# Another order of the matmuls in an attention step, V stored token by token, early stores on ScalarE's queue

## The chip, the cores and the metric

The kernel runs on one core of a Trainium2 chip. The metric is device time in microseconds (us) for one launch. A profiled execution adds a trace: when each instruction ran on TensorE (PE, with its weight loads PEld), VectorE (DVE), ScalarE (ACT), GpSimd (POOL), and when SyncE (SP) issued DMAs. PEclk in its rows is the share of TensorE's full clock that was granted.

## The reference

One transformer block on 2048 tokens of width 512, in float32: a layer norm whose scale and shift come from a condition vector, softmax attention with 32 heads of 16 elements, a second layer norm, and a GELU layer of width 1792.

```python
mod = (silu(c) @ w_mod).reshape(1, 6, 1, -1)
sa, ca, ga, sb, cb, gb = ...
h = layernorm(x) * (1 + ca) + sa
q, k, v = split_heads(h @ wqkv)                     # 32 heads of 16
p = softmax(einsum("bhqd,bhkd->bhqk", q, k) * 16 ** -0.5)
x = x + ga * (einsum("bhqk,bhkd->bhqd", p, v) @ wo)
h = layernorm(x) * (1 + cb) + sb
x = x + gb * (gelu(h @ w1 + b1) @ w2 + b2)
```

## The kernel before

Tokens come in four row blocks of 512 (`NB`, `TB`), heads in eight groups of four (`NG`). A unit `u` is one group of heads with one row block of queries, 32 in all. Every operand of a matmul is split into a rounded part ("hi") and the rest ("lo"), and the products hi·hi, lo·hi and hi·lo are added; for the heads these three products lie under each other in 48 rows of a tile (`KR`), and two further rows add minus the row's maximum, so that the exponent of a score is ready when its matmul ends. A tile has two row halves: rows 0 to 49 belong to one head (a = 0), rows 64 to 113 to another (a = 1).

The order of the work on each engine is written out by hand; the program is issued in just that order.

1. **First part** (`for b in range(NB)`, L489 to L525). Per row block: layer norm, transposes, the q and k projections of the first two groups (`proj_qk`, L294), and half of the V projections (`proj_v`, L323). Results are stored to DRAM, since the attention reads them in another layout. In `proj_qk`, ScalarE copies the hi part, VectorE subtracts the lo part, and for every second block the sums and differences of neighbouring k blocks (`pm`, `pmh`) are made and finished on GpSimd. The stores (L314, L319, L332) are issued on SyncE's queue at once, in order with SyncE's loads. The tiles `parts` and `pmh` share a ring of three buffers. Between the blocks stand the products with the modulation weights (`mod_rows`), whose 1 MB pieces SyncE loads (`load_wm`, L139).
2. **Projections with maxima** (`for n, (k, b, w) in enumerate(items)`, L550). 8 more V items and 24 q or k items, each of 12 matmuls. From the third item on (`FILL0 = 2`) four visits are spread over an item's matmuls; each visit makes two slots of `pair_slot` (L402): two matmuls for the two row halves into a bank each of the ring `mx`, then either an absolute value on ScalarE (V slots) or a sum with minimum on VectorE (U slots). This gives the row maxima of units 0 to 7 from sums and differences of k (`kpm`). Slots that the items don't reach are made after the loop (L582).
3. **Steps** (`for s in range(NS)`, L805). 512 steps; a step is one unit and 128 of its keys. PSUM's eight banks are then the rings `sc` (4), `mx` (3) and `pv` (1). A step does what `ORDER[s % 2]` lists: X0 to X3 are the scores of the four heads (`exp_step`, L794: one matmul in row half j % 2 into a bank of `sc`, then an exponent on ScalarE); P is the product of the step before with V (`pv_step`, L629: four matmuls in four column groups, eight rows in the trace); M0 and M1 are each a bank of maxima for a later unit (`next_max`, `max_bank`, L389: one matmul in row half 0 or 1 into a bank of `mx`, then a maximum over 512 scores on VectorE). `EXTRA` puts a further M at the end of some steps. Units 8 to 31 get their maxima so. When a unit's 64 banks are done, `max_rows` (L429) transposes the result through one more bank of `mx`, and a DMA brings it into the score's extra rows.
4. **Rest** (L834 to the end). Output projection, second layer norm, and the GELU layer.

## Time and profile before

| | us |
|---|---|
| median of 3 runs (lowest to highest) | 1953.41 (1939.52 to 1955.21) |
| the profiled execution | 1953.68 |
| its span | 1951.9 |
| busy PE / DVE / ACT / POOL | 1908.6 / 1444.5 / 1345.3 / 256.3 |
| first part, up to the first matmul of maxima | 0 to 112.31 |
| projections with maxima | 112.31 to 304.75 |
| slots after the loop, up to the first score | 304.75 to 318.98 |
| steps | 318.98 to 1594.6 |
| rest | 1594.6 to 1951.9 |

Busy is the time in which an engine ran an instruction of the program. Matmuls overlap in the array, so a busy PE need not be PE at its peak; in the steps what counts is how many matmuls share it. In the rows of a timeline the first number is the start, the second how long the row lasted; "x3" joins three like instructions, and the bracket at the end holds the engine's idle time before it and what ended it. A row of the view by stages gives for each engine the busy time and the number of instructions, then the granted clock, the DMA engines' busy share and GB/s.

### The profile page before, as it was taken

The numbers are of one execution on the slowest core, as the hardware profiler recorded it, in microseconds if no ns is written. First come the engines' busy times: TensorE is split into PE (matmuls) and PEld (weight loads), VectorE is DVE, ScalarE is ACT, GpSimd is POOL, SyncE is SP. The second block draws the span as 40 slices with busy tenths as digits, with TensorE's granted clock in tenths as the row PEclk, the third lists the DMA queues.
The fourth block names the chain that finished last, engine by engine and source line by source line (L and its number), as shares of the span: only waits on it lengthen the run. The fifth ranks groups of instructions, "written<-read, shape, count | busy, mean of one in ns | idle before, by whom it ended". The sixth has DMA issues, their size and how long they took to land.

```text
span 1951.9 us, 29242 instructions
## 1 busy us (share of the span) xinstructions
PE 1908.6 (98%) x10586; PEld 988.4 (51%) x10586; DVE 1444.5 (74%) x2591; ACT 1345.3 (69%) x2552; POOL 256.3 (13%) x259
## 2 busy tenths in 40 slices
PE   8879999999999999999999999999999999999998
PEld 6535554444444444444444444444444357878887
DVE  6349997588888888888888888888888549566553
ACT  3357776588888888888888888888888853122222
POOL 3200000010000000000000000000001006455562
PEclk9979996699999999999999999999999999999999
DMA  8796445220401301220140011011001315343331
GB/s 248 199 135 145 106 148 93 42 49 26 67 23 29 67 21 24 56 40 21 27 72 20 21 40 26 21 35 31 21 21 58 100 62 173 96 126 92 115 119 54
DMA packets 116800, 139.96 MB, mean 72 GB/s; under 512 B 33104, under 2 KB 67920, under 8 KB 114896
## 3 DMA queue, kind: packets, MB, share of 16 engines
q1 hardware_dynamic: 116656, 138.10, 29.5%
q8 instruction: 83, 1.36, 0.3%
q14 instruction: 61, 0.50, 0.1%
HBM read 104.28 MB, written 33.77 MB: 71 GB/s over the span
## 4 chain that ended last, share of the span: by engine, by line
PE 88%; DVE 5%; DMA 4%; issue 2%; POOL 1%; ACT 0%; SPq 0%; DVEq 0%; POOLq 0%; ACTq 0%
PE pv L635 26%; PE mx L397 22%; PE sc L802 14%; PE sc L290 12%; PE mx L867 5%; PE mx L414 4%; PE pv L867 2%; PE sc L742 1%; DVE mxs L399 1%; DMA wmod<-in_w_mod_dram 1%; DMA kt<-kpm 1%; DMA rb<-rden 1%; DMA kpm<-pmh 1%; PE mx L742 1%; DVE cp L425 0%
## 5 line engine op out<-in xcount | busy, mean ns | idle before, releaser
L803 ACT ACTIVATE p<-sc 128x512 f32<-128x512 f32 x2048 | 1058.4, 606 | 210.8 <-PE sc L802 191.0
L399 DVE TENSOR_REDUCE mxs<-mx 128x1 f32<-128x512 f32 x1536 | 968.9, 684 | 235.5 <-PE sc L802 169.3
L635 PE MATMUL pv<-p,vg 128*32 128x512 f32 x4096 | 557.3, 616 | 0.0
L802 PE MATMUL sc<-qst,kq 50*128 50x512 f32 x1024 | 315.0, 448 | 0.4 <-DVE mr L438 0.4
L397 PE MATMUL mx<-kt,qmx 48*128 48x512 f32 x768 | 312.3, 449 | 1.4
L397 PE MATMUL mx<-kq,qmx 48*128 48x512 f32 x768 | 305.3, 434 | 2.0 <-DVE mxs L399 0.8
L802 PE MATMUL sc<-qst,kt 50*128 50x512 f32 x1024 | 304.9, 430 | 0.0
L397 PEld LDWEIGHTS mx<-kt,qmx 48*128 48x128 f32 x768 | 143.2, 193 | 251.6 <-DVE mxs L399 207.6
L397 PEld LDWEIGHTS mx<-kq,qmx 48*128 48x128 f32 x768 | 138.4, 185 | 244.5 <-DVE mxs L399 218.1
L846 ACT ACTIVATE g<-sc,b_c 128x512 f32<-128x512 f32 x56 | 38.6, 690 | 237.1 <-PE sc L290 228.5
L425 DVE CUSTOM_DVE_ANT_0 cp<-mx,cp 128x512 f32<-128x512 f32 x256 | 164.3, 685 | 33.8 <-PE mx L414 31.3
L440 POOL CAST m<-mr 16x128 fp32r<-16x128 f32 x32 | 9.1, 285 | 1301.6 <-DVE mr L438 1301.6
L421 ACT ACTIVATE cp<-mx 128x512 f32<-128x512 f32 x256 | 140.3, 597 | 57.5 <-PE mx L414 55.3
L635 PEld LDWEIGHTS pv<-p,vg 128*32 128x32 f32 x4096 | 81.6, 108 | 180.1 <-issue 168.5
L802 PEld LDWEIGHTS sc<-qst,kq 50*128 50x128 f32 x1024 | 147.3, 192 | 37.2 <-ACT p L803 21.4
L802 PEld LDWEIGHTS sc<-qst,kt 50*128 50x128 f32 x1024 | 142.7, 185 | 14.2
L850 DVE TENSOR_TENSOR glo<-g,ghi 128x512 fp32r<-128x512 f32 x56 | 60.1, 1073 | 94.8 <-ACT ghi L849 94.8
L414 PE MATMUL mx<-kt,qmx 48*128 48x512 f32 x512 | 102.7, 472 | 11.2 <-DMA qmx<-qk 11.0
L671 POOL TENSOR_TENSOR w1l<-w1r,w1h 128x512 fp32r<-128x512 f32 x56 | 76.8, 1372 | 152.6 <-DVE w1h L670 132.5
L290 PE MATMUL sc<-hThi,w 128*128 128x512 f32 x256 | 82.7, 434 | 3.1 <-DVE hThi L258 3.1
L673 POOL TENSOR_TENSOR w2l<-w2r,w2h 128x512 fp32r<-128x512 f32 x56 | 81.1, 1449 | 6.5 <-DVE w2h L672 6.1
L414 PEld LDWEIGHTS mx<-kt,qmx 48*128 48x128 f32 x512 | 43.9, 192 | 62.9 <-issue 23.7
(147 smaller groups left out, 1646.0 us busy)
## 6 DMA issues: line engine op xcount, KB each, us to landing
qk<-parts SPq DMA_DIRECT2D x32, 512.0 KB
w1r<-in_B_w_dram SPq DMA_DIRECT2D x56, 256.0 KB
w2r<-in_B_w_dram SPq DMA_DIRECT2D x56, 256.0 KB
qmx<-qk SPq DMA_DIRECT2D x192, 64.0 KB
qst<-qk SPq DMA_DIRECT2D x192, 64.0 KB
wmod<-in_w_mod_dram SPq DMA_DIRECT2D x6, 1024.0 KB
kq<-qk SPq DMA_DIRECT2D x24, 256.0 KB
kt<-qk SPq DMA_DIRECT2D x24, 256.0 KB
```

The source lines that it names most:

```text
L290: te.matmul(ps, p, q, start=i == 0, stop=i == len(terms) - 1)
L397: te.matmul(ps, qmx[u][rows, p, qc * P : (qc + 1) * P], kst[u // NB][rows, p, kr * TB : (kr + 1) * TB], start=True, stop=True)
L399: ve.tensor_reduce(mxs[u][:, p, a, qc, kr : kr + 1], ps, axis=AX.X, op=ALU.max, negate=True)
L414: te.matmul(ps, qmx[u][rows, p, qc * P : (qc + 1) * P], kpm[u // NB][rows, p, t0 : t0 + TB], start=True, stop=True)
L421: ac.activation(vabs[n, a], ps, AF.Abs)
L425: ve.tensor_tensor_reduce(v, ps, v, -0.5, 3.0e38, ALU.add, ALU.min, mxs[u][:, p, a, qc, r : r + 1])
L635: te.matmul(cur_pv[0][32 * j : 32 * (j + 1)], vg[g][:, kc, j * VW : j * VW + 32], pt.pop((s, j)), start=kc == 0, stop=kc == NKC - 1)
L671: gp.tensor_tensor(alo, a, ahi.bitcast(F32), op=ALU.subtract)
L673: gp.tensor_tensor(blo, b, bhi.bitcast(F32), op=ALU.subtract)
L802: te.matmul(ps, k[r0 : r0 + KX, p, kc * P : (kc + 1) * P], q[r0 : r0 + KX, p], start=True, stop=True)
L803: ac.activation(pb, ps, AF.Exp, scale=SCALE)
L867: te.matmul(acc[qb][t], p[:, sl], q, start=f == 0 and n == 0, stop=f == NF - 1 and n == 2)
```

## The change

- `ORDER` is rewritten. Both versions have, in two steps, eight X, two P and three M for each row half; they stand in another order.
- The extra M of `EXTRA` now stands behind X1 instead of at the end of the step, one step earlier, and takes its bank from the ring `sc` (written "m0", "m1") instead of `mx`.
- The stores of the first part go to ScalarE's queue (`st[0] = ac`), until item 1 of the second loop, from where they go to SyncE's again. Each is issued one projection later than it was: `proj` keeps the store (`rest`) and issues it after the next projection's own instructions.
- `parts` and `pmh` share four buffers instead of three.
- V lies in DRAM as token, group, element instead of group, token, element. A store of 128 tokens is one run of 2656 bytes for each partition, before eight of 332; the load of a group (`load_v`) is 16 runs of 332 bytes for each partition, before one of 5312.
- `load_qm(0)` stands ahead of the loads of the first `kpm` tile instead of behind them; the second half of that tile is loaded in one place behind the loop; the second `kpm` tile is loaded at item 8 instead of 3.
- Visits begin at item 4 (`FILL0 = 4`), and odd items hold five visits.

```diff
-FILL0 = 2
+FILL0 = 4
-ORDER = ("X0 X1 M0 X2 M0 X3 P M1".split(), "X0 X1 M1 X2 M1 X3 P M0".split())
-EXTRA = {5: 0, 13: 1, 17: 1, 25: 0}
+ORDER = ("X0 X1 M1 X2 M0 X3 P M1".split(), "X0 X1 X2 M0 M0 X3 P M1".split())
+EXTRA = {4: "m0", 12: "m1", 16: "m1", 24: "m0"}
...
-    v_d = dram.tile([NG, P, NKC, VG], F32, name="v")
+    v_d = dram.tile([P, NKC, NG, VG], F32, name="v")
...
+    st = [ac]
...
-        parts = tpool.tile([P, 2, TB], FR, tag="parts", name="parts", bufs=3)
+        parts = tpool.tile([P, 2, TB], FR, tag="parts", name="parts", bufs=4)
...
-            sy.dma_start(qk_d[w][k][:, :, b * TB : (b + 1) * TB].rearrange("a p t -> p a t"), parts.bitcast(F32))
+            st[0].dma_start(qk_d[w][k][:, :, b * TB : (b + 1) * TB].rearrange("a p t -> p a t"), parts.bitcast(F32))
...
-                    sy.dma_start(kpm_d[:, :, t0 : t0 + TB].rearrange("a p t -> p a t"), pmh[i].bitcast(F32))
+                    st[0].dma_start(kpm_d[:, :, t0 : t0 + TB].rearrange("a p t -> p a t"), pmh[i].bitcast(F32))
...
-        return lambda: sy.dma_start(v_d[:, :, b * 4 + t, :].rearrange("g p e -> p g e"), v)
+        return lambda: st[0].dma_start(v_d[:, b * 4 + t], v)
...
-        ps = bank_mx()
+        ps = bk()
...
+    rest = lambda: None
+    def proj(f, *args):
+        nonlocal rest
+        r = f(*args)
+        rest()
+        rest = r
...
             kpm[0], kpm[1] = kts
+            load_qm(0)
             build_k(kts[0], kpm_d, 0, 0, 2 * TB)
...
-        proj_qk(b, 0, 1)()
-        proj_qk(b, 0, 0)()
+        proj(proj_qk, b, 0, 1)
+        proj(proj_qk, b, 0, 0)
         if b == NB - 1:
-            build_k(kts[0], kpm_d, 0, 2 * TB, S)
-            load_qm(0)
             break
...
-    close(acm)
+    build_k(kts[0], kpm_d, 0, 2 * TB, S)
...
-        sy.dma_start(vg[g], v_d[g])
+        sy.dma_start(vg[g], v_d[:, :, g])
...
     for n, (k, b, w) in enumerate(items):
-        if n == 3:
+        if n == 1:
+            close(acm)
+            st[0] = sy
+        if n == 8:
             build_k(kts[1], kpm_d, 1)
...
-            fill = [lambda rest=rest: (rest(), visit()), visit, visit, visit]
+            fill = [lambda rest=rest: (rest(), visit())] + [visit] * (3 + n % 2)
...
-        order = ORDER[s % 2] + [f"M{a}" for k, a in EXTRA.items() if k % 16 == kc and (k < 16 or u < 4)]
+        order = list(ORDER[s % 2])
+        for k, tok in EXTRA.items():
+            if k % 16 == kc and (k < 16 or u < 4):
+                order.insert(2, tok)
...
-                new += next_max(int(tok[1]))
+                new += next_max(int(tok[1]), bank if tok[0] == "m" else bank_mx)
```

More of the change, by code (lines that the diff above doesn't have):

```diff
@@ L307, in proj_qk @@
             pm = [apool.tile([P, TB], F32, tag="h32", name="pm", bufs=3) for _ in range(2)]
-            pmh = [tpool.tile([P, 2, TB], FR, tag="parts", name="pmh", bufs=3) for _ in range(2)]
+            pmh = [tpool.tile([P, 2, TB], FR, tag="parts", name="pmh", bufs=4) for _ in range(2)]
             for i, op in enumerate((ALU.add, ALU.subtract)):
@@ L387, in block_kernel, with max_bank @@
     mi = [NU1 * NM, NU1 * NM]
-    def max_bank(u, i, a):
+    def max_bank(u, i, a, bk):
         if u not in left:
@@ L447, in max_rows, with next_max @@
         return rest
-    def next_max(a):
+    def next_max(a, bk=bank_mx):
         u, i = divmod(mi[a], NM)
@@ L456, in next_max @@
         mi[a] += 1
-        max_bank(u, i, a)
+        max_bank(u, i, a, bk)
         return [] if left[u] else [max_rows(u)]
@@ L513, in block_kernel @@
             mrow = mod_rows(wms)
-        proj_v(*vitems.pop(0))()
+        proj(proj_v, *vitems.pop(0))
         ev = ln1_t(b + 1, xn)
         ev()
-        proj_v(*vitems.pop(0))()
+        proj(proj_v, *vitems.pop(0))
         if b == 1:
@@ L523, in block_kernel @@
         if b == 0:
-            proj_v(*vitems.pop(0))()
-            proj_v(*vitems.pop(0))()
-    close(acm)
+            proj(proj_v, *vitems.pop(0))
+            proj(proj_v, *vitems.pop(0))
+    build_k(kts[0], kpm_d, 0, 2 * TB, S)
     open_psum(sc=2, mx=6)
@@ L540, in block_kernel @@
     slots += [("U", 16 * NU1 - n) for n in (2, 1)]
-    led, todo, rest = 0, [], lambda: None
+    led, todo = 0, []
     new = []
```

## The prediction

> **What bounds the kernel now.** I read the page from the top: span, busy time, granted clock by slices, the chain that ended last.
>
> ```profile
> span 1951.9 us, 29242 instructions
> PE 1908.6 (98%) x10586; PEld 988.4 (51%) x10586; DVE 1444.5 (74%) x2591; ACT 1345.3 (69%) x2552; POOL 256.3 (13%) x259
> PEclk9979996699999999999999999999999999999999
> PE pv L635 26%; PE mx L397 22%; PE sc L802 14%; PE sc L290 12%; PE mx L867 5%; PE mx L414 4%; PE pv L867 2%; PE sc L742 1%; DVE mxs L399 1%; DMA wmod<-in_w_mod_dram 1%; DMA kt<-kpm 1%; DMA rb<-rden 1%; DMA kpm<-pmh 1%; PE mx L742 1%; DVE cp L425 0%
> ```
>
> The chain runs over TensorE, and three lines of the steps (P at L635, M at L397, X at L802) are 62% of it. Then the stages, a row each:
>
> ```profile
> 86.06:112.31 26.25, 12.62 (x53) 9.50 (x52) 2.58 (x4) 4.35 (x8) 3.75 (x3) 0.81 0.90 182
> 112.31:122.80 10.49, 10.49 (x28) 5.42 (x28) 3.56 (x11) 5.61 (x11) 0.00 (x0) 0.50 1.08 136
> 122.80:304.75 181.95, 181.77 (x819) 92.81 (x817) 165.16 (x499) 141.29 (x264) 9.49 (x16) 1.00 0.58 128
> 304.75:318.98 14.23, 11.36 (x35) 4.94 (x35) 13.54 (x44) 9.38 (x17) 0.73 (x2) 0.58 0.10 38
> 318.98:378.80 59.82, 59.82 (x210) 25.08 (x210) 29.81 (x46) 29.75 (x57) 0.73 (x2) 0.50 0.53 73
> 378.80:1516.90 1138.10, 1134.78 (x7096) 480.88 (x7094) 933.61 (x1521) 976.60 (x1900) 37.18 (x62) 1.00 0.16 35
> ```
>
> In the steps at full clock PE is never idle, ACT 86% and DVE 82% busy. Before them lie a stretch with PE half idle (86 to 112), one bound by DVE (304.75 to 318.98), and two at half clock. To see what a step is made of, I take one, PE's rows first, then VectorE's and ScalarE's:
>
> ```profile
> 803.03 0.50 PE L397 MATMUL mx<-kq,qmx 48*128 48x512 f32 x1
> 803.03 0.83 PE L802 MATMUL sc<-qst,kt 50*128 50x512 f32 x3
> 803.61 0.40 PE L397 MATMUL mx<-kq,qmx 48*128 48x512 f32 x1
> 803.85 0.39 PE L802 MATMUL sc<-qst,kt 50*128 50x512 f32 x1
> 804.08 0.39 PE L397 MATMUL mx<-kq,qmx 48*128 48x512 f32 x1
> 804.39 1.06 PE L635 MATMUL pv<-p,vg 128*32 128x512 f32 x8
> 805.39 0.50 PE L397 MATMUL mx<-kq,qmx 48*128 48x512 f32 x1
> 803.57 1.89 DVE L399 TENSOR_REDUCE mxs<-mx 128x1 f32<-128x512 f32 x3 [0.47 <-PE sc L802]
> 803.80 3.73 ACT L803 ACTIVATE p<-sc 128x512 f32<-128x512 f32 x7 [0.49 <-PE sc L802]
> ```
>
> From 803.03 to 805.39 is one step, 2.36 us: 1.00 for P (804.39 to 805.39) and 1.36 for seven matmuls in **five slots**. The first slot is 0.34 long (the block of three covers two slots: 0.83 is 0.34 and a matmul of 0.49), the others 0.23 to 0.24, and 0.31 lie between the last start and P. Two matmuls share a slot where they are neighbours in the program and in different row halves. Write the order between two P as halves. Even step: M0 left over, X0 X1 M0 X2 M0 X3 is 0 0 1 0 0 0 1, so M0 | X0 X1 | M0 | X2 | M0 X3: five. Odd step: M1, X0 X1 M1 X2 M1 X3 is 1 0 1 1 0 1 1, so M1 X0 | X1 | M1 X2 | M1 | X3: five. The names within PE's rows can be swapped, but who takes the results agrees: DVE has its first maximum at 803.57, ACT its first score only a slot later, at 803.80, as M0 | X0 X1 has it.
>
> **The change part by part.** Everything is set against the profiled execution: 1953.68 us, 1.8 beside the span, 0.3 above the median 1953.41.
>
> *The order of the steps.* Even: M1, X0 X1 M1 X2 M0 X3 is 1 0 1 1 0 0 1: M1 X0 | X1 | M1 X2 | M0 X3. Odd: M1, X0 X1 X2 M0 M0 X3 is 1 0 1 0 0 0 1: M1 X0 | X1 X2 | M0 | M0 X3. **Four slots each.** The trace has such a step near the end, where the maxima run out:
>
> ```profile
> 1532.86 0.49 PE L397 MATMUL mx<-kq,qmx 48*128 48x512 f32 x1
> 1532.87 0.73 PE L802 MATMUL sc<-qst,kq 50*128 50x512 f32 x3
> 1533.43 0.39 PE L397 MATMUL mx<-kq,qmx 48*128 48x512 f32 x1
> 1533.67 0.40 PE L802 MATMUL sc<-qst,kq 50*128 50x512 f32 x1
> ...
> 1534.99 0.50 PE L397 MATMUL mx<-kq,qmx 48*128 48x512 f32 x1
> ```
>
> 1532.86 to 1534.99 is 2.13 us: 0.23 less for one slot less (0.235 by the slots' own pitch). There are 1536 banks of maxima on 31 units at 50 (52 in the first four), so they last some 488 steps: 488 x 0.235 = 114.7.
>
> What is late next? ACT's seven exponents in 3.73 contain waits; back to back the eight of the row below take 4.03, so (4.03 - 0.60)/7 = 0.49 each, 1.96 for four. DVE: (1.89 - 0.69)/2 = 0.60, 1.80 for three, 1.88 with the extra M (50 for 16 steps). Both stay under 2.13, with 0.17 and 0.25 spare, so PE remains the bound, barely. Do the rings give banks in time? Score X3's exponent starts at 0.55 + 3 x 0.49 = 2.02 after the step's start and ends 0.60 later, at 2.62; the next X3 goes in at 2.13 + 0.34 + 2 x 0.235 = 2.94. The last M0 starts with it in slot 4 at 0.81, its maximum, third in DVE's line, at 0.54 + 2 x 0.60 = 1.74, ends at 2.43; it is next wanted three M on, at 2.94 in the odd step. So no wait of its own.
>
> ```profile
> 319.87 4.03 ACT L803 ACTIVATE p<-sc 128x512 f32<-128x512 f32 x8 [4.96 <-PE sc L802]
> 806.75 1.07 PE L635 MATMUL pv<-p,vg 128*32 128x512 f32 x8
> 809.45 0.64 PE L635 MATMUL pv<-p,vg 128*32 128x512 f32 x4
> ```
>
> *The extra M.* Before, the step with an extra M takes 2.70 (806.75 to 809.45), 0.34 more than plain. After, it takes a fifth bank from the ring of four: X3 must wait for the exponent of X0 of its own step, 0.55 + 0.60 = 1.15 and some 0.1 for the signal, instead of 0.81, so 0.45; the m1, which needs its own slot, waits inside the same 0.45. That is 0.1 more for 70 extras, 7 us. The 24 transposes of `max_rows` find DVE with less spare time: 3 us, between 0 and 24 times one maximum, 14. Steps: -114.7 + 7 + 3 = **-105**.
>
> *The first part.* PE's waits, in its rows:
>
> ```profile
> 56.28 2.12 PE L290 MATMUL sc<-wv,hThi 128*128 128x512 f32 x8 [2.65 <-ACT mrow L211]
> 71.85 1.93 PE L201 MATMUL sc<-wmod,s_m 128*32 128x512 f32 x8 [5.57 <-DMA wmod<-in_w_mod_dram]
> 74.52 1.93 PE L201 MATMUL sc<-wmod,s_m 128*32 128x512 f32 x8 [0.74 <-DMA wmod<-in_w_mod_dram]
> 91.95 2.03 PE L290 MATMUL sc<-wv,hThi 128*128 128x512 f32 x8
> 94.75 2.03 PE L290 MATMUL sc<-wv,hThi 128*128 128x512 f32 x8
> 100.36 0.96 PE L290 MATMUL sc<-wv,hThi 128*128 128x512 f32 x3 [2.65 <-ACT vst L330]
> 112.31 1.33 PE L414 MATMUL mx<-kt,qmx 48*128 48x512 f32 x4 [10.98 <-DMA qmx<-qk]
> 55.14 0.60 ACT L300 ACTIVATE parts<-sc 128x512 fp32r<-128x512 f32 x1 [7.60 <-DMA qk<-parts]
> 62.04 1.38 SPq L139 DMA_DIRECT2D wmod<-in_w_mod_dram  x2
> 46.98 1.92 PE L201 MATMUL sc<-wmod,s_m 128*32 128x512 f32 x16
> 104.38 3.93 SPq L358 DMA_DIRECT2D qmx<-qk  x6
> ```
>
> The 2.65 at 56.28 comes from ACT's 7.60 for a buffer of `parts` still being stored; with four it falls: -2.65. The modulation weights wait at 62.04 in SyncE's queue behind two V stores, though their buffers are free when the products at 46.98 end (48.9). With the stores gone from that queue they start some 13 us sooner, more than the 5.57 + 0.74 that PE waits: -6.3. With that wait goes the slow clock of its products (16 took 1.92 at 46.98, 3.86 here): -1.9.
>
> Then 112.31. It is 20.4 behind the first item of the second loop (91.95). After, four V items come first, 4 x 2.80 = 11.2 (91.95 to 94.75 is one), and three matmuls, 0.7: +12 at the earliest. The last loads to be issued, `qmx` at 104.38, now come first; the last are then those of `kt`, issued just before 104.38 (+12.4). `qmx` landed 4.0 after its last issue (108.31 to 112.31); with as much, `kt` is there at +16.4, and at about +15 with the V stores out of its way. So +15 for +20.4: **-5.4**, between +12 and +20.4 (the DMA engines are 90% busy there, by the first row of the stages). The half clock from 112.31 to 122.80, 10.49 us, came from that idle time: -5.2. Together **-21.5**. In return ScalarE issues 20 stores (0.66 each at most: 3.93 for six at 104.38) and waits in its queue until DVE or GpSimd has made the last part of each. ScalarE's idle time covers it (busy 4.35 of 26.25 in the first of the stages), with the delay of one projection. Uncovered, the copies to `vst` and `mrow` would stand behind a store, and PE behind them: the nearest rows are the two waits of 2.65, so 0 to +5; I take 0.
>
> *Visits.* Before: 187.2 us (181.95 and half of 10.49) for 30 items with 120 visits; 30 x 2.80 for the items leaves 0.86 a visit. After: 28 items, 126 visits: 78.4 + 108.4 = 186.8. **0**, or +3 if DVE limits the items of five visits (DVE 165.16/120 = 1.38 a visit, 6.9 against PE's 7.1). After the loop 4 slots remain of 16, three U slots of nine. That stretch runs at DVE's pace (13.54 busy of 14.23): 18 banks at 0.60, the nearest row, are 10.8, the last reduction, its transpose and the first score 3.4. With 6 banks it is 3.6 + 3.4 = 7.0: **-7.2**.
>
> *V.* Its loads have 16 times the pieces, but DMA is 16% busy in the steps and a load has some 64 steps' time: 0.
>
> *The clock.* The steps start at half clock, as the stages' fifth row has it (0.50 over 59.82 us). Two of P's rows in the chain, start and length:
>
> ```profile
> 331.66 1.86 PE pv L635 x8
> 335.95 1.86 PE pv L635 x8
> ```
>
> A step is 4.29 there, so 59.82 us hold 13.9 steps, each 1.93 longer: 27 us lost. The short tail may still trigger it. It ends about where the first M0 M1 | X0 X1 stands (the extra M of step 13): two shared slots right behind P; every odd step of the new order begins like that. I take **-15**, between 0 and -27.
>
> Sum: 1953.7 - 105 - 21.5 - 7.2 - 15 = **1805**.
>
> **The rivals.**
> 1. *The evacuations become the bound*: 0.17 and 0.25 us of spare time are little, and a late bank stalls all of PE's queue. For it: the step at 806.75 already pays 0.34 though it needs one slot of 0.235 at most. Against: the ring times above. Priced at half the slot given back, 488 x 0.12 = 59: **1864**. The Trainium skill (TensorEngine Tiling (Array Packing), PSUM Bottleneck) warns of just this, that sharing the array speeds up TensorE but not the emptying of PSUM; ACT's 1.96 and DVE's 1.88 bear that out as the next limit.
> 2. *The half clock ends at once*, since dense shared slots count as busy: 2 or 3 steps of it, so -24 instead of -15: **1796**. For: it ended before at just such a step. Against: 59.82 us of a busy PE had not ended it till then. The Trainium skill (TensorE: Matmul & The Clock Gate, Part 1) has full clock return after about 3.4 us of sustained work; by it the time would be this rival's, but here PE was 100% busy for 59.82 us at 0.50, so the trace does not bear it out for these steps.
> 3. *The first part gains nothing*: its stores only change queue and DMA is 90% busy: **1826**. Against: DMA is late there because it starts late (62.04).
> 4. *Sharing fails*, the change doesn't do what it says: 1953.7 - 21.5 - 7.2 - 15 = **1910**. Against: every pair of the new order but X1 X2 shares a slot already.
> 5. *Slower: the half clock stays.* A four-slot step at half clock is 4.29 - 2 x 0.235 = 3.82, 1.69 above one at full clock. Without the clock's 15 the gain is 134, so from 134/1.69 = 79 such steps beyond today's 14 (some 350 us) the kernel is slower; 120 beyond give 1820 + 203 = **2023**. Against: TensorE is denser than in the steps of 378.80 to 1516.90, which held 1.00.
>
> **How the numbers follow.** Forecast 1805: 0.52; rival 1: 0.13, rival 2: 0.17, rival 3: 0.11, rival 4: 0.04, rival 5: 0.03. The low end is the forecast with all 27 us of clock (-12), the data in time (-3) and no cost of extras and transposes (-10): 1780. The high end is rival 1 at 1864; 4 and 5 are left out. Three runs of the kernel before lie within 0.8%, so about 1% is what can be told from no change. Faster by over 1%: all but rival 5 and a little, 0.95; within 1%: 0.01; slower: 0.04.
>
> **What would show it.** A plain step's P to P at 2.13 (2.2 or more: rival 1, with DVE or ACT ahead of PE in the waits; 2.36: rival 4). ACT over 90% busy in the steps. No wait for the modulation weights, first L414 near 96, first score near 290, the steps shorter by 105 to 120. PEclk at 6 in fewer slices (none: rival 2; many: rival 5). It is wrong above all if the ring times above miss a wait that comes in every step.

## The result, and the profile after

The changed kernel takes **1823.15 us** (median of four runs, 1821.31 to 1849.07) where the kernel before takes 1954.31 beside it. The ratio is **0.9349, with a 95% interval from 0.9282 to 0.9416**: 6.5% less time. Ratios leave out executions over 1.5% longer than the fastest of their kernel (here 2041.82 before and 1849.07 after). The forecast was 1805. The profiled execution took 1821.31 us, 16 more than the forecast: of the 148.7 us that were forecast, 132.4 came, and this part of the document is about the 16 us and about why the rest came.

The page of the changed kernel, its span, PE's line, the granted clock by slices and the chain that ended last:

```profile
span 1819.2 us, 29305 instructions
PE 1789.6 (98%) x10586; PEld 918.0 (50%) x10586; DVE 1441.4 (79%) x2591; ACT 1343.2 (74%) x2552; POOL 256.0 (14%) x259
PEclk9989998999999999999999999999999999999999
PE pv L649 28%; PE mx L400 20%; PE sc L816 14%; PE sc L290 13%; PE mx L884 5%; PE mx L417 5%; PE pv L884 2%; PE sc L756 2%; DMA kt<-kpm 1%; DMA rb<-rden 1%; PE mx L756 1%; DVE glo L867 0%; POOL w2l L687 0%; PE mx L439 0%; PE sc L252 0%
```

PE is as busy as before, 98%, and the chain still runs over the three lines of the steps. The slices at 6 (before: the seventh and eighth) are gone; two at 8 are left, the third and the seventh. The stages, with the columns start:end, length, busy time of PE, of the weight loads, DVE, ACT and POOL, then granted clock, DMA share and GB/s:

```profile
73.89:101.91 28.02, 19.30 (x79) 14.56 (x78) 2.58 (x4) 5.07 (x9) 3.77 (x3) 0.90 0.77 175
101.91:109.89 7.98, 7.94 (x19) 4.03 (x19) 2.24 (x7) 4.73 (x9) 0.00 (x0) 0.50 0.58 194
...
301.30:318.10 16.80, 15.85 (x61) 7.23 (x61) 9.26 (x18) 9.07 (x18) 0.73 (x2) 0.50 0.79 99
318.10:1340.00 1021.90, 1021.80 (x6953) 410.81 (x6952) 913.01 (x1486) 953.66 (x1859) 27.63 (x53) 1.00 0.19 39
```

The stretch at half clock in which the steps begin has shrunk from 71.7 us (307.1 to 378.8) to 17.1 (301.0 to 318.1); 59.8 and 15.5 us of it lie in the steps. In the steps ACT is now 93% busy (953.66 of 1021.90) and DVE 89%, and PE has something in flight for 1021.80 of the 1021.90 us. Some of PE's rows (start, length, operation, in brackets the idle time before it and who ended that):

```profile
79.77 2.03 PE L290 MATMUL sc<-wv,hThi 128*128 128x512 f32 x8
96.05 0.59 PE L417 MATMUL mx<-kt,qmx 48*128 48x512 f32 x1 [4.21 <-DMA kt<-kpm]
101.91 1.56 PE L417 MATMUL mx<-kt,qmx 48*128 48x512 f32 x2 [4.22 <-DMA kt<-kpm]
301.81 0.38 PE L439 MATMUL mx<-ident,mn 128*16 128x128 f32 x1 [3.13 <-DVE mn L435]
302.63 0.97 PE L816 MATMUL sc<-qst,kq 50*128 50x512 f32 x2 [0.44 <-DVE mr L441]
...
560.25 0.49 PE L400 MATMUL mx<-kq,qmx 48*128 48x512 f32 x1
560.25 0.72 PE L816 MATMUL sc<-qst,kt 50*128 50x512 f32 x3
560.82 0.40 PE L400 MATMUL mx<-kq,qmx 48*128 48x512 f32 x2
561.05 0.40 PE L816 MATMUL sc<-qst,kt 50*128 50x512 f32 x1
561.38 1.07 PE L649 MATMUL pv<-p,vg 128*32 128x512 f32 x8
562.38 0.50 PE L400 MATMUL mx<-kq,qmx 48*128 48x512 f32 x1
```

From 560.25 to 562.38 is one step, 2.13 us; from P to P the median of all steps is 2.125, and it was 2.361. The first five rows show the visits starting at 96.05, where the forecast had them, but stopping after one pair for the second half of `kt`. Set against the forecast by these starts (the last projection before the steps starts at 303.55 before and at 294.72 after, the last P ends at 1595.9 and at 1462.9):

| stretch | before | after | difference | forecast |
|---|---|---|---|---|
| start to the first V item of the second loop | 91.95 | 79.77 | -12.2 | -10.9 |
| from there until the visits run (112.31; 101.91) | 20.4 | 22.1 | +1.8 | -5.4 |
| from there to the last projection | 191.2 | 192.8 | +1.6 | -5.2 |
| from there to the first score | 15.4 | 7.9 | -7.5 | -7.2 |
| the steps | 1276.9 | 1160.2 | -116.7 | -120 |
| the rest | 356.0 | 356.3 | +0.3 | 0 |

Two rows of the table hold 14 of the 16 us: the second and the third. In the first row, 1.8 us lie ahead of the first V product (28.50 before, 26.69 after). Other traces have it anywhere from 26.4 to 30.1 us, so that part is chance; counted from the first V product, the row is 63.4 and 53.1, or -10.4.

### The profile page after: what moved, and what is told of

Its sections match the earlier page's. It is cut to its first block, busy times and chain, and to the rows that moved or that the text cites. A ratio compares the mean times of both kernels' runs of the same rounds, so it can differ in the third digit from the quotient of the medians.

```text
span 1819.2 us, 29305 instructions
## 1 busy us (share of the span) xinstructions
PE 1789.6 (98%) x10586; PEld 918.0 (50%) x10586; DVE 1441.4 (79%) x2591; ACT 1343.2 (74%) x2552; POOL 256.0 (14%) x259
## 4 chain that ended last, share of the span: by engine, by line
PE 91%; DVE 3%; DMA 2%; issue 2%; POOL 1%; ACT 0%; SPq 0%; ACTq 0%; DVEq 0%; POOLq 0%
PE pv L649 28%; PE mx L400 20%; PE sc L816 14%; PE sc L290 13%; PE mx L884 5%; PE mx L417 5%; PE pv L884 2%; PE sc L756 2%; DMA kt<-kpm 1%; DMA rb<-rden 1%; PE mx L756 1%; DVE glo L867 0%; POOL w2l L687 0%; PE mx L439 0%; PE sc L252 0%
## 5 line engine op out<-in xcount | busy, mean ns | idle before, releaser
L402 DVE TENSOR_REDUCE mxs<-mx 128x1 f32<-128x512 f32 x1467 | 930.6, 685 | 118.6 <-PE sc L816 81.5
L649 PE MATMUL pv<-p,vg 128*32 128x512 f32 x4096 | 548.6, 607 | 0.0
L816 PE MATMUL sc<-qst,kq 50*128 50x512 f32 x1024 | 298.3, 445 | 0.5 <-DVE mr L441 0.4
L816 PE MATMUL sc<-qst,kt 50*128 50x512 f32 x1024 | 293.1, 436 | 0.0
L400 PE MATMUL mx<-kq,qmx 48*128 48x512 f32 x738 | 260.4, 429 | 1.3 <-DVE mxs L402 1.1
L400 PE MATMUL mx<-kt,qmx 48*128 48x512 f32 x729 | 259.5, 432 | 0.0
L400 PEld LDWEIGHTS mx<-kq,qmx 48*128 48x128 f32 x738 | 122.0, 184 | 224.2 <-DVE mxs L402 204.1
L400 PEld LDWEIGHTS mx<-kt,qmx 48*128 48x128 f32 x729 | 122.7, 187 | 219.2 <-DVE mxs L402 202.2
L816 PEld LDWEIGHTS sc<-qst,kq 50*128 50x128 f32 x1024 | 132.4, 187 | 44.7 <-ACT p L817 35.2
L816 PEld LDWEIGHTS sc<-qst,kt 50*128 50x128 f32 x1024 | 130.9, 185 | 21.9 <-ACT p L817 14.4
L417 PE MATMUL mx<-kt,qmx 48*128 48x512 f32 x512 | 102.7, 459 | 9.1 <-DMA kt<-kpm 8.7
L417 PEld LDWEIGHTS mx<-kt,qmx 48*128 48x128 f32 x512 | 48.2, 186 | 61.8 <-issue 32.0
```

The costliest lines, as they stand in the source:

```text
L400: te.matmul(ps, qmx[u][rows, p, qc * P : (qc + 1) * P], kst[u // NB][rows, p, kr * TB : (kr + 1) * TB], start=True, stop=True)
L402: ve.tensor_reduce(mxs[u][:, p, a, qc, kr : kr + 1], ps, axis=AX.X, op=ALU.max, negate=True)
L417: te.matmul(ps, qmx[u][rows, p, qc * P : (qc + 1) * P], kpm[u // NB][rows, p, t0 : t0 + TB], start=True, stop=True)
L649: te.matmul(cur_pv[0][32 * j : 32 * (j + 1)], vg[g][:, kc, j * VW : j * VW + 32], pt.pop((s, j)), start=kc == 0, stop=kc == NKC - 1)
L816: te.matmul(ps, k[r0 : r0 + KX, p, kc * P : (kc + 1) * P], q[r0 : r0 + KX, p], start=True, stop=True)
```

## The experiments

Eleven kernels, in three groups: what the parts of the change give, why two products share a slot, and where the half clock comes from. Ratios are to the kernel before, run beside each; the changed kernel's is 0.9349. The four buffers, the stores' delay by one projection, the new order of the loads and the later visits were not run alone.

### The order of the steps alone, on the kernel before

```diff
-ORDER = ("X0 X1 M0 X2 M0 X3 P M1".split(), "X0 X1 M1 X2 M1 X3 P M0".split())
+ORDER = ("X0 X1 M1 X2 M0 X3 P M1".split(), "X0 X1 X2 M0 M0 X3 P M1".split())
```

> The kernel before with the new ORDER alone; the extra M stay at the end of their steps in the ring mx, everything ahead of the steps is as before. Theory (two matmuls share a slot when they are program neighbours in different row halves): plain steps 2.12 instead of 2.36, the steps 97 us shorter, and as the half clock ends within some 4 steps because of the new order, 20 more: 1954 - 117 = 1837. Rival on the clock (it ended early because the stretch ahead of the steps was shorter): half clock for some 60 us again, 1857. Rival on the order (the gain came from the banks of the extra M): 1954.

Measured: 1843.75 us (1840.41 to 1848.49), ratio 0.9462, from 0.9390 to 0.9534: 105 us of the 127 that the whole change gives by its ratio. The median step is 2.125 as in the changed kernel, an extra M makes it 2.70, and the half clock in which the steps begin lasts 20.5 us instead of 71.7. So one line carries five sixths of the change, a part of it by the clock; the rival on the clock (1857) and the one on the banks of the extra M (1954) did not come.

### Everything but the order and the extra M

```diff
-ORDER = ("X0 X1 M1 X2 M0 X3 P M1".split(), "X0 X1 X2 M0 M0 X3 P M1".split())
-EXTRA = {4: "m0", 12: "m1", 16: "m1", 24: "m0"}
+ORDER = ("X0 X1 M0 X2 M0 X3 P M1".split(), "X0 X1 M1 X2 M1 X3 P M0".split())
+EXTRA = {5: "M0", 13: "M1", 17: "M1", 25: "M0"}
...
-                order.insert(2, tok)
+                order.append(tok)
```

> The changed kernel with the old ORDER and the old extra M. Theory: only what stands ahead of the first score is gained, 319.0 - 302.6 = 16 us, and the steps start with some 60 us of half clock again: 1938. Rival on the clock (the shorter stretch ahead of the steps ends it): half clock for some 15 us, 1938 - 20 = 1918.

Measured: ratio 0.9919, from 0.9837 to 1.0002, 16 us, an interval that reaches no change. The ratio rests on the three shortest of ten runs (1919.24 to 1941.16); the median of all ten, 1961.50, is no shorter than the 1955.15 beside it. The profiled execution took 1963.92, so only its stages are compared: the first score stands at 309.9, 9 earlier than before, and the median step is 2.361. The runs scatter from 1919.24 to 2000.59 us, and the scatter is the half clock: the granted clock of a whole run goes from 0.988 in the shortest to 0.945 in the longest, some 46 and 220 us at half clock, which cost half as much. A window of the profiled execution, with the columns of the stages above:

```profile
310.00:409.00 99.00, 99.00 (x348) 40.49 (x349) 49.44 (x77) 49.27 (x94) 2.61 (x5) 0.50 0.43 62
```

PE is busy in all of 99 us and runs at half clock in all of them. The stretch is 102.4 us long here and 71.7 in the kernel before, with the same steps; what ends it is not known. In the six traces with the new order in which nothing fills PE's waits it is over after 10 to 21 us, which is a second gain of the order. These are single executions: the changed kernel's longest, 1849.07, had a granted clock of 0.972 where the profiled one had 0.991, some 70 us more at half clock. So long ones occur with the new order too; where in the kernel is not known.

### V in the old layout, on the changed kernel

```diff
-    v_d = dram.tile([P, NKC, NG, VG], F32, name="v")
+    v_d = dram.tile([NG, P, NKC, VG], F32, name="v")
...
-        return lambda: st[0].dma_start(v_d[:, b * 4 + t], v)
+        return lambda: st[0].dma_start(v_d[:, :, b * 4 + t, :].rearrange("g p e -> p g e"), v)
...
-        sy.dma_start(vg[g], v_d[:, :, g])
+        sy.dma_start(vg[g], v_d[g])
```

> The changed kernel with V laid out in memory group by group, as it was before the change. Theory: the layout is of no account, because no row of the first part waits for a V store's or a V load's length itself: 1823, within 1814 to 1832, first visit near 96 us, first score near 303. Rival: writing a token's groups in one piece is what makes the transfers between 88 and 102 us end sooner; then the third visit comes later than 101.9 by 2 us or more and the time is 1826 to 1832.

Measured: 1839.83 us (1835.93 to 1847.75), ratio 0.9422, from 0.9377 to 0.9467. This was a miss, beyond the rival's 1826 to 1832 too: the layout was expected to be of no account, and the visits begin 8 us later (104.1; they run from 109.3), 2 of them ahead of the first V product (28.82); the first score stands at 312.3. The longest of PE's waits ahead of the second loop, and the window from 40 to 60 us of this kernel:

```profile
60.63 0.74 PE L290 MATMUL sc<-hThi,w 128*128 128x512 f32 x2 [3.11 <-DVE hThi L258]
40.00:60.00 20.00, 17.53 (x97) 13.30 (x95) 6.37 (x14) 4.79 (x8) 3.54 (x3) 1.00 0.97 197
```

The same window of the changed kernel:

```profile
40.00:60.00 20.00, 19.31 (x102) 14.04 (x100) 10.12 (x24) 8.43 (x14) 6.08 (x5) 1.00 0.72 255
```

With the old layout the DMA engines are full (0.97) and move less (197 GB/s for 255). The modulation weights are issued at 48.42 here, as early as in the changed kernel (47.16) and 13 us sooner than before (62.04), and PE no longer waits for them. But they take 10.4 us to land, and ScalarE stands for that from 52.85 to 58.88, ahead of a store whose landing is told by the same semaphore (more on that below); so its copies for the next block, and with them `hThi` and PE (3.11), come late. A V store of 332 KB is then cut into 128 x 8 pieces of 332 bytes; with the new layout a partition's eight pieces lie together, and the short pieces are in the loads of V, during the steps, where the engines are 19% busy. The Trainium skill (DMA: Bandwidth & Descriptors, Specifications) has 512 bytes as the least transfer that runs at line rate; the two windows agree with that.

### V's new layout alone, on the kernel before

```diff
-    v_d = dram.tile([NG, P, NKC, VG], F32, name="v")
+    v_d = dram.tile([P, NKC, NG, VG], F32, name="v")
...
-        return lambda: sy.dma_start(v_d[:, :, b * 4 + t, :].rearrange("g p e -> p g e"), v)
+        return lambda: sy.dma_start(v_d[:, b * 4 + t], v)
...
-        sy.dma_start(vg[g], v_d[g])
+        sy.dma_start(vg[g], v_d[:, :, g])
```

> The kernel before with one edit: V laid out in memory token by token, as the changed kernel has it. Theory, from the run with the old layout: storing V in short pieces fills the DMA engines in the first part (0.97 to 1.01 of them busy from 40 to 60 us at about 200 GB/s), and the modulation weights and the rows of x wait for that; in the new layout the short pieces are in the loads, where the engines are idle. So the wait of 5.57 before the products of the modulation weights falls to under 2, the first visit comes 6 to 12 us before 112.3, the share from 40 to 60 falls below 0.85, and the time is 1940 to 1948. Rival, the prediction's: those weights wait for their place in SyncE's queue behind V stores that wait for their data; then a wait of about 5 stays with the new layout, the first visit is at 110 or later and the time is 1952 to 1957.

Measured: ratio 0.9914, from 0.9863 to 0.9964, 17 us (median 1942.67), as the theory had it. The first visit comes at 102.16, 10.2 before 112.31; counted from the first V product (26.44) it is 8.1. PE's waits in this kernel from 54 us to the visits:

```profile
62.43 1.07 PE L201 MATMUL sc<-wmod,s_m 128*32 128x512 f32 x8 [0.84 <-DVE xin L270]
65.14 1.94 PE L201 MATMUL sc<-wmod,s_m 128*32 128x512 f32 x8 [1.64 <-DMA wmod<-in_w_mod_dram]
90.09 0.96 PE L290 MATMUL sc<-wv,hThi 128*128 128x512 f32 x3 [2.13 <-ACT vst L330]
102.16 1.31 PE L414 MATMUL mx<-kt,qmx 48*128 48x512 f32 x4 [11.10 <-DMA qmx<-qk]
```

Its window from 40 to 60 us:

```profile
40.00:60.00 20.00, 20.00 (x108) 15.48 (x107) 12.06 (x28) 9.14 (x15) 8.52 (x7) 1.00 0.68 235
```

The wait of 5.57 for the modulation weights is down to 1.64, and the 2.65 for `mrow` at 56.28 is gone, though `parts` still has three buffers and every store still goes through SyncE's queue. So most of the gain ahead of the second loop is the layout's. From the first V product to the first V item of the second loop it takes 63.4 us before, 55.8 with the layout alone, 59.6 with all of the change but the layout, and 53.1 with all of it: 7.7 by the layout alone, 3.9 by the rest alone, 10.4 together. The 11.10 before the first visit is as it was.

### All stores on SyncE's queue, on the changed kernel

```diff
-    st = [ac]
+    st = [sy]
```

> The changed kernel with all stores on SyncE's queue, still one projection later. Theory: the modulation weights wait behind the stores again, some 13 us later than now, so PE waits about 6 us and runs some us at half clock: 1827 to 1835. Rival (the queue is of no account, the four buffers and the layout of V made the gain): 1821.

Measured: 1823.21 us (1813.72 to 1832.20), ratio 0.9362, from 0.9291 to 0.9433: no difference to the changed kernel, as the rival had it. Inside, two differences work against each other. The row of PE where the visits begin to run:

```profile
96.00 0.50 PE L417 MATMUL mx<-kt,qmx 48*128 48x512 f32 x1 [2.76 <-DMA kt<-kpm]
```

The window behind it:

```profile
96.00:131.00 35.00, 34.73 (x86) 16.51 (x86) 15.70 (x48) 16.96 (x32) 0.00 (x0) 0.51 0.22 80
```

The visits run from 96.00, not from 101.91, since both halves of `kt` are there; but the half clock behind the wait lasts 34.1 us instead of 13.7, and the first score stands at 309.0. (This profiled execution is the longest of the four, 1832.20; the half clocks of the others are not known.) In the changed kernel SyncE's own queue shows why `kt` is late, from 60 to 100 us (who waited for what: us in total, times, longest):

```profile
SPq L361 <- DMA v<-vst: 5.7, 1, 5.7
SPq L386 <- DMA v<-vst: 4.8, 1, 4.8
```

A load on SyncE's queue waits until a V store *that ScalarE issued* has landed: the transfers of both queues share the semaphores that tell of their landing, and a new one waits for its turn of the same semaphore. In the trace the load of `qmx` waits for the very semaphore that it will raise itself; the V store issued at 79.81 raises it for the last time at 82.07, and the load is issued at 82.08. So the stores were taken out of SyncE's queue and not out of its way.

### The last V store of the third block issued before the loads

```diff
         if b == NB - 1:
+            rest()
+            rest = lambda: None
```

> The changed kernel with the last V store of block 2 issued at the top of block 3, ahead of the loads of the ones, qmx and kpm, instead of behind the next projection. Theory: SyncE's loads there wait for a semaphore that the V store shares; issued some 7 us sooner, the 5.7 us wait of the second qmx load is gone, the first visits run 5 to 6 us sooner and with less or no half clock behind them: 1811 to 1816. Rival (the kpm stores behind GpSimd set the time): 1821.

Measured: 1825.50 us (1817.48 to 1831.72), ratio 0.9372, from 0.9306 to 0.9437: no gain. SyncE's queue in this kernel, the same view:

```profile
SPq L361 <- DMA qk<-parts: 5.7, 1, 5.7
```

The wait for V's store is gone and the next load waits just as long, 5.7, for the store of `parts` whose turn comes next (landed at 84.81, load issued at 84.83); the visits run from 102.81. One late store less only passes the turn on.

### The extra M at the end of its step, in the maxima's ring

```diff
-EXTRA = {4: "m0", 12: "m1", 16: "m1", 24: "m0"}
+EXTRA = {5: "M0", 13: "M1", 17: "M1", 25: "M0"}
...
-                order.insert(2, tok)
+                order.append(tok)
```

> The changed kernel with each extra product of maxima at the end of its step and in the maxima's own ring, as before the change, instead of third in the step and in the scores' ring. By slots, an extra product of the first half of the rows stands beside the step's last product, of the other half, and costs nothing; one of the second half costs 0.235; the mean is 0.12 for some 70 of them where 0.52 was measured: -28, so 1795. Theory: the three banks of the maxima's ring give a bank in time (fourth reduction of the step ended 3.6 us after the step's start, wanted at 4.1), so most of that comes: 1797 to 1805. Rival: four reductions at 0.60 are 2.40 for a step of 2.12, VectorE falls behind and the ring makes PE wait at least as long as now: 1823 or more.

Measured: 1834.38 us (1832.06 to 1845.48), ratio 0.9400, from 0.9350 to 0.9450; the theory missed and the rival's side came. A step with an extra M takes 2.70, whichever half it is of, where the changed kernel's takes 2.64. The slots have no part in it, or M0 and M1 would differ.

### Products of one half next to each other

```diff
-ORDER = ("X0 X1 M1 X2 M0 X3 P M1".split(), "X0 X1 X2 M0 M0 X3 P M1".split())
+ORDER = ("X1 M1 X3 X0 X2 M0 P M1".split(), "X0 X1 X2 M0 M0 X3 P M1".split())
```

> The changed kernel with the even step written X1 M1 X3 X0 X2 M0 P M1: the same products of each half of the rows, but products of one half stand next to each other. Theory: only neighbours in the program share a slot of 0.235 us, so the even step has 6 slots instead of 4, +0.47 on half of some 488 steps: +115, 1936 (even steps 2.59, odd steps 2.12). Rival: each half of the rows runs its own products in order, whatever stands between them, and the step lasts as long as its fuller half: no change, 1823, to 1835 with waits for banks.

Measured: 1894.12 us (two runs, 1880.08 and 1908.16), ratio 0.9695, from 0.9560 to 0.9830: between the two, so the steps decide. An even step takes 2.22, an odd one 2.12, a step with an extra M 3.08. An even step in PE's rows, from P to P, and below them three exponents on ScalarE:

```profile
565.08 1.06 PE L649 MATMUL pv<-p,vg 128*32 128x512 f32 x8
566.07 0.50 PE L400 MATMUL mx<-kq,qmx 48*128 48x512 f32 x1
566.16 0.99 PE L816 MATMUL sc<-qst,kt 50*128 50x512 f32 x3
566.65 0.40 PE L400 MATMUL mx<-kq,qmx 48*128 48x512 f32 x1
566.89 0.40 PE L816 MATMUL sc<-qst,kt 50*128 50x512 f32 x1
566.99 0.40 PE L400 MATMUL mx<-kq,qmx 48*128 48x512 f32 x1
567.32 1.06 PE L649 MATMUL pv<-p,vg 128*32 128x512 f32 x8
565.03 1.57 ACT L817 ACTIVATE p<-sc 128x512 f32<-128x512 f32 x3
```

Between the two P stand seven products, 1 1 1 1 0 0 0 by halves, of which only one pair are neighbours: six slots, some 1.6 us, if neighbours alone could share. They take 1.25, from 566.07 to 567.32, 0.10 more than the alternating order. The second start follows the first by 0.09, and two of one half are never closer than 0.23, so this must be one of half 0, the first of which stands four places further on in the program. **Each half of the rows works through its own products; the fuller half between two P sets the time.** The old order had five of one half between two P (M0, X0, M0, X2, M0, or M1, X1, M1, M1, X3), the new one four and three, and over two steps both have seven and seven: so P is a barrier, and what counts is the count between two of them. The 0.10 is a wait for ScalarE: the second start, 566.16, and the fourth, 566.65, come 0.05 after an exponent has ended (566.11 and, by its row, 566.60), and over 132 such steps the medians are 0.05 as well. Those two products wait for a bank of the scores. The Trainium skill says both things: that tiles operate independently (TensorEngine Tiling (Array Packing), Key Properties), with which these rows agree, and that matmuls start and end in strict program order (TensorE: Matmul & The Clock Gate, Part 3), by which the even step would have been near the 2.59 of six slots; the measured 2.22 is against that.

Of the 51 us by which the steps are longer than the changed kernel's, some 145 plain even steps make 15; the other 38 or so stand in the 68 steps with an extra M (0.44 more for each) and behind the ends of units (0.3 more). Why grouping makes those dearer is open.

### Seven slots in two steps

```diff
-ORDER = ("X0 X1 M1 X2 M0 X3 P M1".split(), "X0 X1 X2 M0 M0 X3 P M1".split())
+ORDER = ("X0 X1 X2 M0 X3 P M1".split(), "X0 X1 M0 M1 X2 X3 M0 P M1".split())
```

> The changed kernel with the steps X0 X1 X2 M0 X3 P M1 and X0 X1 M0 M1 X2 X3 M0 P M1: the same products in two steps, but the fuller half has 3 of them in one stretch between two P and 4 in the next, 7 slots in two steps instead of 8; its neighbours pair to the same 7. By slots alone two steps take 4.25 - 0.235 = 4.02, which is 57 us less: 1766. By the banks of the maxima: four of them start in one stretch of 0.94 us, and the fourth needs the bank of the first, whose reduction ends 0.54 + 0.60 after its start, some 0.3 to 0.45 later than its slot; two steps take 4.3 to 4.5, and the time is 1840 to 1880. I hold the second.

Measured: 1914.72 us (two runs), ratio 0.9810, from 0.9716 to 0.9904, slower than expected by both: two steps take 4.59, where the banks were to make it 4.3 to 4.5. PE's rows, three P and what is between:

```profile
856.83 1.07 PE L649 MATMUL pv<-p,vg 128*32 128x512 f32 x8
857.82 0.49 PE L400 MATMUL mx<-kq,qmx 48*128 48x512 f32 x1
857.83 1.01 PE L816 MATMUL sc<-qst,kq 50*128 50x512 f32 x4
858.39 0.39 PE L400 MATMUL mx<-kq,qmx 48*128 48x512 f32 x1
858.77 1.07 PE L649 MATMUL pv<-p,vg 128*32 128x512 f32 x8
859.77 0.49 PE L400 MATMUL mx<-kq,qmx 48*128 48x512 f32 x1
859.77 0.72 PE L816 MATMUL sc<-qst,kq 50*128 50x512 f32 x2
860.11 0.62 PE L400 MATMUL mx<-kq,qmx 48*128 48x512 f32 x2
860.34 0.66 PE L816 MATMUL sc<-qst,kq 50*128 50x512 f32 x2
861.04 0.50 PE L400 MATMUL mx<-kq,qmx 48*128 48x512 f32 x1
861.47 0.64 PE L649 MATMUL pv<-p,vg 128*32 128x512 f32 x4
```

The step with three in the fuller half is a slot shorter, as counted: the median is 1.89, 0.235 under 2.125. The one with four of each half takes 2.70: its fourth M starts at 861.04, 1.27 after the first (859.77), when the first one's bank is free (start, 0.54 until the reduction can begin, 0.60 of reduction, and the signal); P follows 0.43 later. So the step is set by two counts between two P: the products of the fuller half, and the maxima, of which a fourth must wait for a bank of the ring of three. Two maxima and three slots make 1.89, three maxima and four slots 2.12, four maxima and four slots 2.70. That is also the extra M: four maxima stand between two P in each step that has one, and such steps take 2.70 in the kernel before and wherever all four use the ring of three. In the changed kernel, where the fourth takes a fifth bank from the scores' ring of four, they take 2.64. That this wait is the scores' own shows here: a step with an extra M has only three maxima in this order and takes 2.64 as well.

### Products that nobody reads, in PE's waits

```diff
+WARM_V, WARM_X = (18, 18), 13
...
+    def warm_fill(n):
+        ps = bank_mx()
+        for i in range(n):
+            te.matmul(ps, hT[0][0][:, 0, :P], hT[0][0][:, 1], start=True, stop=True)
...
+        if kind == "V" and n < 2:
+            warm_fill(WARM_V[n])
...
+    warm_fill(WARM_X)
     for f in todo:
         f()
```

> The changed kernel with products that nobody reads in three waits of PE: 18 full-array products of 0.23 us in each of the two waits of 4.2 us before the first and the third visit, 13 in the wait of 3.1 us before the last transpose ahead of the steps. Theory: the half clock comes from those idle microseconds, so the stretches at 0.50 (96.2 to 109.9 and 301.0 to 318.1) do not appear; that gives about 4 us in the first part and 4 steps at 2.12 instead of 3.87, 7 us: 1812, within 1808 to 1818. Rival: the half clock comes with the change to products in half of the rows, whether PE idled before or not: stretches at 0.50 as now, 1823 to 1826.

Measured: 1820.01 us (1817.41 to 1824.59), ratio 0.9318, from 0.9271 to 0.9365. In the changed kernel the three windows from the first wait into the steps are:

```profile
91.00:103.00 12.00, 3.24 (x8) 1.39 (x6) 0.00 (x0) 0.00 (x0) 0.00 (x0) 0.72 1.03 156
103.00:110.00 7.00, 7.00 (x18) 3.49 (x17) 2.35 (x7) 4.73 (x9) 0.00 (x0) 0.51 0.50 159
301.00:318.00 17.00, 15.75 (x61) 7.13 (x61) 9.46 (x18) 8.97 (x18) 0.73 (x2) 0.50 0.76 96
```

With the unread products:

```profile
91.00:103.00 12.00, 11.29 (x47) 8.31 (x45) 0.00 (x0) 0.00 (x0) 0.00 (x0) 1.00 1.04 134
103.00:110.00 7.00, 6.57 (x24) 3.26 (x25) 2.81 (x9) 4.98 (x10) 0.00 (x0) 1.00 0.67 226
301.00:318.00 17.00, 16.46 (x106) 7.04 (x105) 14.49 (x24) 14.82 (x29) 0.73 (x2) 1.00 0.86 109
```

Both half clocks are gone, at the same change to half-row products: PE's idle microseconds cause them. The gain is smaller than the 11 us expected. The steps' start gains 5.5 (the first unit 40.73 to 36.01, and 0.8 ahead of its first P), the first part 1 (3 counted from the first V product, 28.68 here), and a half clock of 10.2 us at 1368 gives 4 of it back (that unit 37.64 to 41.83): there PE waits 1.00 for VectorE, and in the changed kernel's profiled execution 1.13, with no half clock behind it; another of 3.4 follows at 1580. What decides whether a wait of one microsecond brings one is open.

### All of it together

```diff
-EXTRA = {4: "m0", 12: "m1", 16: "m1", 24: "m0"}
+WARM_V, WARM_X = (13, 1), 13
+EXTRA = {5: "m0", 12: "m1", 16: "m1", 25: "m0"}
...
-    st = [ac]
+    st = [sy]
...
+        if kind == "V" and n < 2:
+            warm_fill(WARM_V[n])
...
+    warm_fill(WARM_X)
...
-            at(s0 + (12 if qb else 6) + 2 * k + d, lambda qb=qb, k=k, i=i: o_norm(qb, k)[i]())
+            at(s0 + (12 if qb else 8) + 2 * k + d, lambda qb=qb, k=k, i=i: o_norm(qb, k)[i]())
...
-                order.insert(2, tok)
+                order.insert(order.index("P") + 1, tok)
```

> The changed kernel with what the runs point to: all stores on SyncE's queue, 13 unread products before the first visit and before the last transpose ahead of the steps, the extra products behind P (one of the first half in an odd step, one of the second half in an even step, where the fuller half still has four between two P) and the products of the first block's normalisation two steps later, so that VectorE doesn't stand behind them near 1365 us. Against 1820 of the run with unread products alone: the visits begin 6 earlier and the projections before them 1 later (-5); an extra step takes 2.4 to 2.55 instead of 2.64 (-6 to -15, since the fifth product from the ring of four still makes one score wait); no half clock near 1368 (-4 to -6). 1795 to 1806; rival, each of these is hidden behind the next limit: 1812 to 1822.

Measured: 1818.14 us (1812.61 to 1833.49, six runs), ratio 0.9325, from 0.9268 to 0.9382. The clock on its page, and PE's line:

```profile
PE 1792.5 (99%) x10613; PEld 926.4 (51%) x10613; DVE 1442.9 (80%) x2591; ACT 1342.4 (74%) x2552; POOL 256.1 (14%) x259
PEclk9999999999999999999999999999999999999999
```

The rival's 1812 to 1822 came, not the 1795 to 1806. In the profiled execution (1812.61, the shortest of the six) no slice is below 9; three stretches of 3.4 us at half clock are left, at 11.4, 25.1 and 100.2. The visits run from 95.9, the first score stands at 296.3 (302.6 in the changed kernel), and the wait near 1365 is gone. The extra steps are no shorter (2.70 for 2.64). By the medians that is 5 us under the changed kernel and by the intervals nothing that can be told from it, so there is no version here that surely beats it.

## Why the prediction was right, and where it was wrong

**The order of the steps** (-114.7): right in size, 2.125 for 2.13. Its step "Two matmuls share a slot where they are neighbours in the program and in different row halves" is wrong as a rule: with the halves grouped it asked for six slots and 2.59, and the step took 2.22, of which 0.10 is a wait for a bank. The rule that the rows bear out, the fuller half between two P, gives five for the old order and four for the new one as well. That the number came out is luck: for these two orders both rules count alike.

**The extra M** (0.45 forecast): 0.52, for some 70 steps 5 us more. The cause was named rightly, a bank of the scores that must be waited for. **The transposes** (+3): 2.74 where the plain step is 2.12, so 0.62; before 2.94 over 2.36, 0.58, so 1. Not forecast at all: the step behind each unit's end takes 2.31 instead of 2.12, 31 times 0.19 or 6 us. It was 2.36 in the kernel before, like every other; ACT copies the unit's result there (L636), and with the 0.17 that the prediction found spare in a step that copy shows.

**The clock** (-15, between 0 and -27): four steps at 3.87 instead of 14 at 4.29, 7 us lost instead of 27, so -20. Right in size, but its reason, that the extra M of step 13 ended the half clock, is not borne out: with the same steps it went on for 23 steps without the order and 24 with V's layout alone. What ends it stays open. Together the steps gave -116.7 for -120.

**The first part up to the second loop** (-10.9): -12.2 measured, -10.4 without what lies ahead of the first V product. The number is luck in part, since the causes were credited wrongly. The step was "*V.* Its loads have 16 times the pieces [...]: 0": the loads indeed cost nothing, but nothing was made of the stores, whose pieces become eight times longer at the same time. The buffers (-2.65) and the queue (-6.3 and -1.9) got the credit. The weights did start 13 us sooner, as forecast; but all of the change without the layout gives 3.9 of these us, the layout alone 7.7, with three buffers and with all stores on SyncE's queue, and the queue is worth nothing in the total. What the buffers and the delay give was not run alone.

**The wait for `kt`** (+15 for +20.4, so -5.4): +22.1, so +1.8, a miss of 7.2. The step that went wrong is "at about +15 with the V stores out of its way". On ScalarE's queue they were still in the way, by the semaphores of their landing; with all stores on SyncE's queue the visits run 6 us earlier.

**The half clock behind it** (-5.2) followed that wait: 7.98 us of it are left from 10.49, so -1.2. With the wait filled it disappears; the cause was right, the wait was not gone. **The visits** (0, or +3 if DVE limits the items of five visits): the third row of the table less that 1.2 is +2.8. The odd items take 7.3 to 7.5 us, not 7.1: the case that was put second came. **The tail** (-7.2): -7.5.

So 16 us: 7.2 by `kt`, 4.0 by its half clock, 2.8 by the visits and 3.3 by the steps, and 0.3 by the rest, less 1.6 gained in the first and the fourth row.

**The rivals.** Evacuations as the bound (1864) did not come: a plain step takes the 2.125 that its four slots ask for. But they are the next limit, as the order with seven slots shows: there a slot less costs more than it gives. The half clock that ends at once (1796) did not come either: in the traces the half clocks in which the steps begin last 10.2 to 20.5 us with the new order and 71.7 to 112.6 with the old one, most of it with a busy PE. The 3.4 us of the Trainium skill (TensorE: Matmul & The Clock Gate, Part 1) are not borne out for products in half of the rows. Sharing that fails (1910) and a half clock that stays (2023) are excluded by 2.125 and by the slices of the clock. The first part that gains nothing (1826) was near in time for another reason: it gained 8.8 of its 21.5 (the table's first three rows).

## What to carry to other kernels

Here, products in different row halves ran as two streams between two products that need all rows: count each half's share between two such products, and the results that must leave PSUM in the same stretch, and move products until both counts are least. Before moving a store to another queue, look at the size of its pieces and at who waits for its landing: the layout was worth some 17 us here, in both runs that change it alone, and the queue nothing. When PE waits some microseconds, what follows may run at half clock much longer than the wait (34.1 us behind one of 2.76), so price a wait with what comes behind it.

## What the runs showed of the hardware that was not expected

What ends the half clock is not known. With the old order it lasted 71.7, 102.4 and 112.6 us in three traces, with PE busy in all of the 59.8, 99.5 and 103.9 us of them that lie in the steps; with the new one 10.2 to 20.5 us. All these lengths are whole multiples of 3.41 us (3 to 6, and 21, 30 and 33). It makes the scatter of the kernels with the old order (1919 to 2001 us for one of them).

A DMA's semaphore can tie queues together, as this program gives them out: a load on SyncE's queue waited 5.7 and 4.8 us for stores on ScalarE's queue with which it shares no data but a semaphore, and when one store was issued sooner the same 5.7 went to the next.

A product runs ahead of three others of the other half that precede it in the program (starts 0.09 us apart at 566.07 and 566.16).
